# Loading K and Q in six-token runs: cast during the load, transposed head by head, written back in token order by the evacuation

## The chip, the cores and the metric

The kernel runs on one core of one Trainium2 chip. The metric is device time in microseconds (us), and each kernel is given as the median of several executions. All ratios below compare executions in the fast state; a median is taken over all executions of a run, so now and then a slow one is in it. (A slower state was seen in some executions of several of the kernels, the kernel before among them: on one chip 289.27 us in it, against 284.91 to 288.84 in its fast ones.) The engines are PE (matmul; PEld is its weight load), DVE, ACT and POOL (the vector, scalar and general engines), and SP, which here only issues DMA transfers. The kernel keeps its tiles in two on-chip memories, SBUF and PSUM. PE's results are in PSUM (`Sps`, `Ops` and `Mps` in the traces); the loads go to tiles in SBUF. A copy from PSUM to SBUF is called an evacuation.

## The reference, cut to what matters

Block-sparse attention over 4 batches, 8 heads, 768 tokens and 64 elements per head, followed by a gated MLP on the result:

```python
scores = (1 / sqrt(D)) * q @ k.T           # per batch and head, 768 x 768
# mask: blocks of 32 tokens: own block and both neighbours, the first and last
# block as rows and columns, and 3 sampled blocks for each block of queries
attn = softmax(where(mask, scores, -1e9))
x = (attn @ v)                             # heads side by side: 768 x 512
h = gelu(x @ w_in); u, w = halves of h
w = layer_norm(w) * g_ln
out = x + (u * (w_sg @ w + b_sg)) @ w_out
```

Inputs and output are float32, and q, k and v are 0.1 times a standard normal draw. The scores are therefore close to zero and the softmax close to a plain mean over the allowed tokens. A result that agrees with the reference says little about the order of the tokens in Q and K.

## The kernel before

The program is written as a list of operations with their reads and writes and a modelled duration (`dur`). A list scheduler with a model of the chip puts them in an order for each engine before the kernel is built. The program fixes the order: each engine gets its own list, with waits on semaphores.

For each batch, Q and K must end up with the head elements on the partitions (`QT`, `KT`: 128 partitions = 2 heads x 64, 768 tokens along the row), in bf16. The path is load (float32, into one of two staging buffers), cast to bf16 on POOL, six 128x128 transposes on PE into PSUM, evacuation by ACT or DVE:

```python
def load1(b, nm, c, n_, aft=()):                  # one pair of heads (c) of q, k or v
    ...                                           # batches 1-3: stg is one of the two buffers ST
    if nm == "v" or b:                            # 256-byte runs: one token of one head
        sr = SRC[nm][b, 2*c:2*c+2].rearrange("h (t p) d -> p (h t) d", p=P)
        sg = stg.rearrange("p (a d) -> p a d", d=D)
    else:                                         # batch 0, q and k: 512-byte runs, two tokens
        sr = SRC[nm][b, 2*c:2*c+2].rearrange("h (n p j) d -> p (h n) (j d)", p=P, j=2)
        sg = stg.rearrange("p (a d) -> p a d", d=2*D)
    ld = op("SP", ..., lambda e: e.dma_start(sg, sr), ...)
    ...
    eng = CAST0[nm] if b == 0 else CS1 if (b, nm) == (1, "v") else "POOL"
    op(eng, f"cs{nm}{b}.{c}", fn, ...)            # the cast, float32 -> bf16
# [...]
def tr(pe, ...):                                  # transposes of one pair of heads
    for t in range(T):                            # T = 6
        cc = u.slot * 1024 + t * P
        ins = pe.transpose(Mbf[:, cc:cc + P], n_[:, c, t, :], ident[:, :])
# [...]
def ev(x, ...):                                   # evacuation; Q on ACT and K on DVE for b > 0
    src = Mbf[:, u.slot * 1024:u.slot * 1024 + S]
    o_ = TT[:, c, 0:S]
    if b == 0:                                    # two tokens of a run lie side by side in QT/KT
        src = src.rearrange("p (n j c) -> p n j c", n=3, j=2)
        o_ = o_.rearrange("p (n c j) -> p n j c", n=3, j=2)
    return x.activation(o_, src, ACT.Copy) if ee == "ACT" else x.tensor_copy(o_, src)
```

In batch 0 a partition holds two neighbouring tokens. After the transpose these lie in two different blocks of 128 columns, so the evacuation must interleave them: it writes bf16 elements with a stride of 2 elements (4 bytes).

The softmax here doesn't subtract the row's maximum and nothing guards it: scores larger than these inputs give would overflow.

## Time and profile before

| | before |
|---|---|
| time, median of the first 3 executions (with the one beside the changed kernel: 4) | 284.9 us (283.02) |
| span of the profiled execution, granted clock | 280.6 us, 0.95 |
| DMA packets of 256 B, and what they took (mean; sum over 16 engines) | 61,440; 20.7 ns; 79.3 us |
| all DMA packets, time summed and divided by 16 engines | 199.0 us |

The last two rows are sums over the trace's packet records. Here is the head of the page of the kernel before. The first two lines give the span and the busy time of each engine with its share and its instruction count. In the others the span is cut into 40 slices of 7 us; a digit is the busy share in tenths, and PEclk is the granted clock of PE.

```profile
span 280.6 us, 8680 instructions
PE 216.9 (77%) x3525; PEld 159.9 (57%) x3525; DVE 163.8 (58%) x469; ACT 152.4 (54%) x227; POOL 112.4 (40%) x208
...
PE   0134675878776999974588998969669999999974
...
PEclk9999998779999999999689999997959999999999
DMA  8999989999969768588996794868910112320033
```

No engine is full. The DMA row is near 9 for the first third, and the PE row has two dips, near 130 and near 195 us. These are the borders between batches, where PE has to wait for the next Q and K. Busy time per engine in three stretches of 30 us shows the same (first the stretch and its length; then the busy us of PE, PEld, DVE, ACT and POOL, each with its number of instructions in parentheses; then PE's granted clock, the DMA share and GB/s. A packet is counted in the stretch in which it starts, so a DMA share can pass 1):

```profile
60.00:90.00 30.00, 24.78 (x242) 18.34 (x234) 20.02 (x61) 14.06 (x23) 13.42 (x18) 0.94 0.99 214
120.00:150.00 30.00, 19.71 (x220) 14.22 (x212) 16.28 (x53) 13.25 (x21) 16.44 (x21) 0.89 0.93 218
180.00:210.00 30.00, 22.49 (x264) 17.70 (x263) 17.59 (x53) 14.02 (x21) 17.52 (x23) 0.83 0.70 178
```

PE's waits by releaser (total us, times, longest) name the cause of those dips. `Mps L591` is the transposes, and `qn`, `kn` are the cast Q and K. The third line is the first score matmul, which waits for an evacuation. (Left out are 13.3 us for batch 0's own casts, at the start, and others.)

```profile
PE Mps L591 <- POOL qn L559: 13.0, 8, 3.0
...
PE Mps L591 <- POOL kn L559: 1.8, 2, 1.2
PE Sps L394 <- ACT QT L604: 1.7, 1, 1.7
```

The casts are late because their staging loads are late: the page has POOL idle for 34.7 us before its 12 casts of K, all of it until a load had landed:

```profile
L559 POOL CAST kn<-ST 128x768 bf16<-128x768 f32 x12 | 10.0, 830 | 34.7 <-DMA ST<-in_k_dram 34.7
```

In the page's chain of waits, which follows the last instruction back to what released it, POOL has 11% and DMA 19%:

```profile
PE 40%; DMA 19%; SPq 12%; POOL 11%; issue 10%; DVE 5%; ACT 2%; POOLq 0%
```

The instructions of the evacuation line are given as minimum/median/maximum in ns, then first and last start in us, then the shapes:

```profile
L604 ACT ACTIVATE QT<-Mps x14: 804/811/1021, 27.8 to 206.6; 128x768 bf16<-128x768 bf16 x14
L604 DVE COPY KT<-Mps x12: 516/558/558, 62.2 to 186.7; 128x768 bf16<-128x768 bf16 x12
L604 ACT ACTIVATE KT<-Mps x4: 1007/1012/1027, 15.8 to 20.7; 128x768 bf16<-128x768 bf16 x4
L604 DVE COPY QT<-Mps x2: 1004/1004/1005, 23.0 to 24.5; 128x768 bf16<-128x768 bf16 x2
```

The last two groups and two of the first belong to batch 0 and write with the 4-byte stride: 1.0 us on both engines. The others write with unit stride: 0.56 us on DVE and 0.81 on ACT.

### The profile page before, as it was taken

The page shows a single profiled execution, that of the slowest core. Times are in us where ns is not written, and L with a number is a line of the kernel's source. Part 1 is how long each engine was busy: PE and PEld are TensorE (multiplying, and loading weights), DVE is VectorE, ACT ScalarE, POOL GpSimd, SP SyncE. Part 2 cuts the span into 40 slices and gives each one's busy share as a digit, 9 for nine tenths or more (in the row PEclk, how much of TensorE's full clock was granted, in tenths as well). Part 3 has the DMA queues.
Part 4 walks back from the last instruction along what each step waited for, and adds up shares of the span by engine and source line. Part 5 has one row for each costly group of instructions (what it writes and reads, how often), then busy time and mean ns, then how long its engine had stood idle before and what let it go on. Part 6 is the DMA issues. An engine that isn't in the chain of part 4 may idle for free.

```text
span 280.6 us, 8680 instructions
## 1 busy us (share of the span) xinstructions
PE 216.9 (77%) x3525; PEld 159.9 (57%) x3525; DVE 163.8 (58%) x469; ACT 152.4 (54%) x227; POOL 112.4 (40%) x208
## 2 busy tenths in 40 slices
PE   0134675878776999974588998969669999999974
PEld 0123454766454677762466676756467777868442
DVE  6108634212986658529254897655934685557783
ACT  3471876845064657750556756745527667766000
POOL 1017863160387865125669543128674220012000
PEclk9999998779999999999689999997959999999999
DMA  8999989999969768588996794868910112320033
GB/s 155 245 279 220 231 189 283 270 204 235 263 116 238 165 148 185 130 208 214 248 208 154 143 211 100 202 165 218 265 31 3 31 45 56 127 66 0 0 114 112
DMA packets 93852, 45.43 MB, mean 162 GB/s; under 512 B 68468, under 2 KB 88084, under 8 KB 93812
## 3 DMA queue, kind: packets, MB, share of 16 engines
q1 hardware_dynamic: 86848, 34.26, 54.5%
q0 software_dynamic: 4128, 9.02, 12.8%
q10 hardware_dynamic: 2836, 1.60, 2.7%
q8 instruction: 28, 0.46, 0.7%
q14 instruction: 12, 0.10, 0.1%
HBM read 36.49 MB, written 9.55 MB: 164 GB/s over the span
## 4 chain that ended last, share of the span: by engine, by line
PE 40%; DMA 19%; SPq 12%; POOL 11%; issue 10%; DVE 5%; ACT 2%; POOLq 0%
PE Mps L394 25%; DMA ST<-in_q_dram 7%; PE Ops L394 6%; POOL VR L678 6%; PE Sps L394 5%; SPq L548 5%; DMA ST<-in_k_dram 5%; DMA scr<-VA 4%; SPq L670 3%; DMA uT<-in_k_dram 3%; DVE gt L979 2%; SPq L632 2%; POOL KR L695 2%; PE Mps L913 2%; POOL qn L559 2%
## 5 line engine op out<-in xcount | busy, mean ns | idle before, releaser
L678 POOL DMA_INDIRECT VR<-scr,IDX x47 | 46.4, 987 | 24.0 <-issue 9.0
L691 DVE COPY KR<-KT 128x128 bf16 x176 | 33.2, 256 | 9.1 <-PE Sps L394 4.7
L394 PE MATMUL Mps<-w_sgT,vh 128*128 128x384 bf16 x192 | 35.1, 327 | 0.2
L695 POOL COPY KR<-KT 128x128 bf16 x88 | 23.5, 308 | 21.2 <-PE Sps L394 21.1
L394 PE MATMUL Mps<-w_out,xg 128*128 128x512 f32 x96 | 29.5, 433 | 1.9 <-DVE xg L982 1.6
L394 PE MATMUL Mps<-w_in,xg 128*128 128x512 f32 x96 | 27.5, 432 | 3.1 <-ACT vg L937 2.1
L979 DVE SCALAR_TENSOR_TENSOR gt<-Mps,gcol,bsg 128x384 f32<-128x384 f32 x32 | 19.7, 617 | 16.2 <-PE Mps L394 15.6
L394 PE MATMUL Mps<-xg,w_in 128*128 128x384 f32 x128 | 28.3, 368 | 0.7 <-ACT uT L964 0.2
L770 ACT ACTIVATE PR<-Sps 96x1024 bf16<-96x1024 f32 (+1 forms) x24 | 22.8, 948 | 8.2 <-PE Sps L394 8.2
L997 DVE TENSOR_TENSOR x_tok<-Mps,x_tok 128x512 f32<-128x512 f32 x24 | 16.6, 690 | 16.3 <-PE Mps L394 16.0
L394 PEld LDWEIGHTS Mps<-xg,w_in 128*128 128x128 f32 x128 | 22.9, 202 | 4.4 <-ACT uT L964 1.8
L937 ACT ACTIVATE vg<-Mps 128x512 f32<-128x512 f32 x24 | 14.2, 597 | 20.0 <-PE Mps L394 18.4
L604 ACT ACTIVATE QT<-Mps 128x768 bf16<-128x768 bf16 x14 | 11.6, 839 | 23.3 <-PE Mps L591 15.3
L394 PEld LDWEIGHTS Mps<-w_sgT,vh 128*128 128x128 bf16 x192 | 17.2, 98 | 11.9 <-DVE gt L979 1.4
L559 POOL CAST kn<-ST 128x768 bf16<-128x768 f32 x12 | 10.0, 830 | 34.7 <-DMA ST<-in_k_dram 34.7
L591 PE MATMUL Mps<-ident,qn 128*128 128x128 bf16 x96 | 9.9, 252 | 17.7 <-POOL qn L559 13.0
L394 PEld LDWEIGHTS Mps<-w_in,xg 128*128 128x128 f32 x96 | 18.0, 202 | 9.0 <-ACT vg L937 3.6
L920 ACT ACTIVATE xg<-Mps 128x512 fp32r<-128x512 f32 x24 | 14.3, 594 | 15.5 <-PE Mps L913 15.3
L394 PEld LDWEIGHTS Mps<-w_out,xg 128*128 128x128 f32 x96 | 17.1, 196 | 7.3 <-DVE xg L982 2.4
L950 DVE TENSOR_SCALAR vh<-vg,lnmv,lny 128x512 bf16<-128x512 f32 x24 | 13.3, 594 | 13.2 <-POOL lny L946 13.2
L964 ACT ACTIVATE uT<-Mps 128x384 f32<-128x384 f32 x32 | 15.7, 492 | 9.7 <-PE Mps L394 9.3
L939 DVE BATCH_NORM_STATS2 lnst<-vg 128x6 f32<-128x512 f32 x24 | 16.3, 679 | 7.8 <-ACT vg L937 7.8
(98 smaller groups left out, 399.7 us busy)
## 6 DMA issues: line engine op xcount, KB each, us to landing
out_dram<-x_tok SPq DMA_DIRECT2D x20, 256.0 KB, 3.4
ST<-in_v_dram SPq DMA_DIRECT2D x12, 384.0 KB
ST<-in_k_dram SPq DMA_DIRECT2D x12, 384.0 KB
ST<-in_q_dram SPq DMA_DIRECT2D x12, 384.0 KB
VR<-scr SPq DMA_DIRECT2D x123, 32.5 KB, 2.9
scr<-VA SPq DMA_DIRECT2D x6, 390.0 KB, 6.9
w_in<-in_moe_w_in_dram POOLq DMA_DIRECT2D x1, 2048.0 KB, 9.6
VS<-scr SPq DMA_DIRECT2D x3, 650.0 KB, 7.5
```

The costliest lines, as they stand in the source:

```text
L394: return pe.matmul(o, l, r, start=start, stop=True, skip_group_check=True)
L559: fn = {"DVE": lambda x: x.tensor_copy(o4, i4), "ACT": lambda a: a.activation(o4, i4, ACT.Copy), "POOL": lambda g: g.tensor_copy(o4, i4)}[eng]
L678: return g.indirect_dma_start(out=VR[0:96, uV.slot, :, :].rearrange("p h e -> p (h e)"), out_offset=None, in_=src[:, :], in_offset=bass.In ...
L691: ins = x.tensor_copy(KR[:, c0:c0 + n, rg, 32 * j:32 * j + 32], KT[:, c0:c0 + n, bass.ds(vals["DVE", i][j][0], 32)])
L695: op("POOL", f"kp{b}.{i}{hh}", lambda x, i=i, rg=rg: x.tensor_copy(KR[:, c0:c0 + n, rg, 64:96], KT[:, c0:c0 + n, bass.ds(vals["POOL"][0][i ...
L770: return lambda a: a.activation(o, i_, ACT.Exp, scale=SCALE)
L920: return x.tensor_copy(o_, i_) if xe == "DVE" else x.activation(o_, i_, ACT.Copy)
L937: op("ACT", f"gV{b}.{tau}", lambda a: a.activation(vg[vr][:, :], Mps[:, u.slot * 512:u.slot * 512 + 512], ACT.Gelu_apprx_tanh), r=[("vp", ...
L939: op("DVE", f"bs{b}.{tau}", lambda x: x.bn_stats(lnst[:, vr, :], vg[vr][:, :]), r=[("vg", vr)], w=[("lnst", vr)], dur=0.73, prio=pr - 300)
L964: o = op("ACT", f"gU{b}.{c}{dt}", lambda a: a.activation(uT[c][:, dt, :], Mps[:, u.slot * 512:u.slot * 512 + 384], ACT.Gelu_apprx_tanh), r ...
L979: op("DVE", f"g1{b}.{c}{dt}", lambda x: x.scalar_tensor_tensor(gt[gr][:, :], Mps[:, u.slot * 512:u.slot * 512 + 384], gcol[:, dt:dt + 1], ...
L997: op("DVE", f"res{b}.{tau}", lambda x: x.tensor_tensor(x_tok[bp][:, tau, :], Mps[:, u.slot * 512:u.slot * 512 + 512], x_tok[bp][:, tau, :] ...
```

## The change

The intent is to remove what the borders wait for. A partition takes six consecutive tokens of a head, so a load reads runs of 6 x 64 x 4 = 1,536 bytes instead of 256. For batches 1 to 3 POOL issues the loads and the DMA casts to bf16 on the way; the staging buffer and POOL's cast of Q and K fall away, and Q and K can arrive an attention early. The layout on the partition is now [head, 6 tokens, 64], so each head is transposed by itself into one half of the PSUM partitions. A column block t of PSUM then holds the tokens 6p + t, and the evacuation has to put them back in token order. The scheduler also gets a table of priority offsets (`OFF`), found by an offline search of the schedule model, and new durations in the model. The core of the diff:

```diff
+OFF = { "TRk0": -456, "TRk1": -1922, ... }         # 223 entries [cut]
-                o.prio = -rk[o.idx] if RANK == 1 else o.prio - RANK * rk[o.idx]
+                o.prio = o.prio - RANK * rk[o.idx] + OFF.get(kind(o), 0)
...
-    qn = sb("qn", [P, 4, T, P], BF16)              # and kn
+    qn = sb("qn", [P, H, T, D], BF16)
...                                                 # batch 0, in load1
-            sr = SRC[nm][b, 2 * c:2 * c + 2].rearrange("h (n p j) d -> p (h n) (j d)", p=P, j=2)
+            sr = SRC[nm][b, 2 * c:2 * c + 2].rearrange("h (p j) d -> p h (j d)", j=T)
...                                                 # batches 1-3, in loads
+            if b and nm != "v":
+                if c % 2 == 0:
+                    z = c // 2
+                    dst = {"k": kn, "q": qn}[nm]
+                    o = op("POOL", f"ld{nm}{b}.{z}", lambda g, ...: g.dma_start(
+                        dst[:, 4 * z:4 * z + 4, :, :].rearrange("p h j d -> p h (j d)"),
+                        SRC[nm][b, 4 * z:4 * z + 4].rearrange("h (p j) d -> p h (j d)", j=T)), ...)
+                continue
...                                                 # transposes, batches 1-3
+                            for hp in range(2):
+                                ins = pe.transpose(Mbf[64*hp:64*hp+64, ...], n_[:, 2*c+hp, t, :], ident[:, :], tile_position=(0, 64 * hp))
...                                                 # evacuation, all batches
-                    src = Mbf[:, u.slot * 1024:u.slot * 1024 + S]
-                    o_ = TT[:, c, 0:S]
-                    if b == 0: [the 4-byte interleave]
+                    src = Mbf[:, u.slot * 1024:u.slot * 1024 + S].rearrange("p (j c) -> p j c", j=T)
+                    o_ = TT[:, c, 0:S].rearrange("p (c j) -> p j c", j=T)
-                op(ee, ..., dur=(0.85 if ee == "ACT" else 0.6) + 0.35 * (b == 0), ...)
+                op(ee, ..., dur=1.0, ...)
```

The evacuation's loop runs over t (j) outside and over the partition (c) inside, so its writes have a stride of six bf16 elements, 12 bytes. The model of the new schedule takes 1.0 us for it.

## The prediction

> **What bounds the kernel now.** No single engine: the page's busy shares are PE 77%, DVE 58%, ACT 54%, POOL 40%. In the table of engine time by stretches the DMA share is about 1.0 from 0 to 80 us, and PE works 45 of those 80: the front is DMA-bound. After 100 us PE sets the pace, except at the batch borders: it is busy 19.7 of 30 us in 120–150 and 22.5 of 30 in 180–210, and the granted clock falls to 0.75 and 0.67 there. PE's waits show why: the transposes waited 13.0 us for POOL's casts of Q and 1.8 us for those of K; POOL's casts waited for the staging loads (34.7 us for K, 16.0 for Q). The chain of waits runs through these loads and casts at 55–62, 85–91, 112–121, 133–138 and 184–206 us.
>
> **What the change does.**
> - K and Q of batches 1–3: 36,864 packets of 256 B, 20.7 ns each in the trace's packet records, 47.6 us of all 16 DMA engines. They become 6,144 packets of 1,536 B in, 768 B out. The casting weight load (1,536 B out) took 144 ns a packet; half of that is an estimate of 72 ns, 28 us in all. Batch 0's K and Q go from 512 B packets (35 ns, 13.6 us) to 1,536 B, about 9–10 us. Together 23 us of 199 us of DMA time. [...] this trace still rises from 512 B (14.5 B/ns per engine) to 2,048 B (21).
> - POOL loses 24 casts of 0.83 us (20 us) and gains 12 load issues of about 0.85 us (as the weight loads), 10 us. The two-buffer staging ring serves V alone, so K and Q can arrive an attention early.
> - Transposes: six 128-wide become twelve 64-wide in two column halves that should overlap; I allow 0 to 0.3 us for each of 24.
> - Evacuations lose their unit stride. Batch 0's strided ones show the price: DVE 1.00 against 0.56 us, ACT 1.01 against 0.81; 5.3 us of DVE and 2.4 us of ACT over 12 each. [...]
> - The new order comes from a model, so part of its promise won't appear.
>
> **On the critical path.** Front 3–5 us (first scores at 29.7 us move to about 26); 60–100 us 4–6 us; border at 120–150 us 7–8 us; border at 180–210 us 5–6 us, some of it clock. Given back: 2–4 us through slower evacuations and transposes. Net about 20 us. The last 20 us (PE and DVE alternating) stay. Floor: PE work of 210 us after a start at 27 us, front bubbles of 9 us and a tail of 5, about 251; I don't expect to reach it.
>
> Predicted: 264 us, 80% range 254 to 275. Faster by over 2%: 0.92; within 2%: 0.06; slower: 0.02.
>
> **What would show it right.** PE's waits for POOL's casts gone and not replaced by waits for the new loads; PE over 26 of 30 us at both borders, clock at least 0.95; 256 B packets down by 36,864; DMA busy time near 176 us; POOL busy down by 10 us; strided evacuations near 1.0 us; first scores near 26 us; PE busy within 5 us of 217.
>
> **What would make it wrong.** Casting loads much slower than 72 ns a packet; POOL issues that delay the gathers; V's path (load, cast, scratch write, gathers) setting the borders by itself; an order fitted to a model that stalls the in-order engines on the chip; PE instruction fetch with 144 more transposes.

Its sum: 3 to 5, 4 to 6, 7 to 8 and 5 to 6 us, less 2 to 4, about 20 us in all.

## The result

| | before | after |
|---|---|---|
| time, median of 4 executions | 283.02 us (280.63 to 284.92) | 300.62 us (300.06 to 301.39) |
| span and granted clock of the profiled execution | 280.6 us, 0.95 | 298.2 us, 0.90 |
| packets of 256 B | 61,440 | 24,576 |
| casting packets of K and Q (768 B written) | none | 6,144, 87.5 ns each |
| all DMA packets, time / 16 | 199.0 us | 176.2 us |
| evacuations of Q and K, summed over the four groups | 24.1 us | 85.4 us |

The ratio of after to before is 1.0704, with a 95% interval of 1.0651 to 1.0758: slower by 7%. Here and below, a ratio is the mean time of one kernel's fast runs over that of the other's of the same rounds, so it is not quite the ratio of the medians quoted beside it.

The head of the page after:

```profile
span 298.2 us, 8924 instructions
PE 225.6 (76%) x3669; PEld 165.8 (56%) x3669; DVE 187.2 (63%) x469; ACT 184.2 (62%) x227; POOL 101.1 (34%) x196
...
PE   0131367863488999977779999958858999999995
...
PEclk9999999995559999996559999975986999999999
DMA  8985593899993788775599471420251102420005
```

DMA and POOL are relieved as planned: POOL is down by 11 us. But ACT is up by 32 us and DVE by 23. The number of DVE and ACT instructions has not changed (469 and 227), so the same instructions have become longer. PE's dips have not gone: the one near 130 us is shallower but longer, the one near 195 us longer too, and there is a new one near 70 us. The clock falls in all of them, to 0.66 over 30 us in two. The stretches around the dips:

```profile
60.00:90.00 30.00, 17.33 (x364) 13.67 (x365) 17.49 (x42) 19.21 (x15) 7.06 (x20) 0.66 1.11 226
130.00:160.00 30.00, 22.68 (x433) 17.09 (x432) 20.97 (x45) 21.26 (x20) 10.99 (x22) 0.66 0.71 132
190.00:230.00 40.00, 30.42 (x547) 23.00 (x546) 26.58 (x59) 25.31 (x28) 12.96 (x25) 0.79 0.30 78
```

PE's waits say for what. No line with POOL's casts is left. (Batch 0's own casts, on ACT and DVE, are left out again: 16.8 us.) Instead PE waits for the evacuations (L651), which hold the PSUM buffers that transposes, scores and the MLP's matmuls write to:

```profile
PE Mps L641 <- ACT QT L651: 6.9, 5, 2.2
PE Mps L641 <- DVE KT L651: 6.7, 4, 1.9
...
PE Mps L960 <- DVE KT L651: 3.9, 3, 1.5
...
PE Mps L960 <- ACT QT L651: 3.1, 2, 1.7
PE Sps L430 <- ACT QT L651: 2.8, 1, 2.8
```

With the three smaller ones (1.9, 1.9, 0.9) these waits are 28.1 us; before, PE waited 2.9 us for evacuations. The chain of waits agrees: ACT and DVE have gone from 7% to 36%, and DMA and POOL from 30% to 9%:

```profile
PE 47%; ACT 18%; DVE 18%; DMA 9%; SPq 3%; issue 3%; ACTq 1%; POOL 0%; DVEq 0%
```

And the evacuation line itself:

```profile
L651 ACT ACTIVATE QT<-Mps x14: 2719/2744/2967, 32.5 to 222.6; 128x768 bf16<-128x768 bf16 x14
L651 DVE COPY KT<-Mps x12: 2697/2786/2867, 65.0 to 201.7; 128x768 bf16<-128x768 bf16 x12
L651 ACT ACTIVATE KT<-Mps x4: 2699/2708/2940, 15.4 to 24.2; 128x768 bf16<-128x768 bf16 x4
L651 DVE COPY QT<-Mps x2: 2694/2700/2705, 27.7 to 31.9; 128x768 bf16<-128x768 bf16 x2
```

They take 2.7 to 2.8 us, on two different engines, where the prediction (and the model of the new schedule) had 1.0. The sum is 37.6 + 31.7 + 10.7 + 5.4 = 85.4 us, 61 us more than before; the forecast was 7.7 us more. The timeline of ACT shows what this does at the first border (start, length, instruction, and in brackets the idle time before it and its releaser):

```profile
75.51 0.85 ACT L595 ACTIVATE VA<-ST 128x768 bf16<-128x768 f32 x1 [9.97 <-DMA ST<-in_v_dram]
...
76.74 10.41 ACT L651 ACTIVATE QT<-Mps 128x768 bf16<-128x768 bf16 x4
```

ACT first sits idle for V's load and then spends 10.4 us on four evacuations in a row, in which nothing else gets through.

### The profile page after: what moved, and what is told of

The parts are those of the page before. It is cut to its first block, busy times and chain, and to the rows that moved or that the text cites. A ratio compares the mean times of both kernels' runs of the same rounds, so it can differ in the third digit from the quotient of the medians.

```text
span 298.2 us, 8924 instructions
## 1 busy us (share of the span) xinstructions
PE 225.6 (76%) x3669; PEld 165.8 (56%) x3669; DVE 187.2 (63%) x469; ACT 184.2 (62%) x227; POOL 101.1 (34%) x196
## 4 chain that ended last, share of the span: by engine, by line
PE 47%; ACT 18%; DVE 18%; DMA 9%; SPq 3%; issue 3%; ACTq 1%; POOL 0%; DVEq 0%
PE Mps L430 29%; ACT QT L651 10%; DVE KT L651 7%; PE Ops L430 7%; DMA ST<-in_v_dram 6%; PE Sps L430 6%; DVE gt L1026 4%; DVE xg L1029 3%; ACT KT L651 3%; PE Mps L960 3%; DMA uT<-in_k_dram 2%; PE Mps L641 2%; ACT PW L818 2%; SPq L584 1%; DVE QT L651 1%
## 5 line engine op out<-in xcount | busy, mean ns | idle before, releaser
L742 POOL COPY KR<-KT 128x128 bf16 x88 | 22.7, 300 | 62.0 <-DVE KT L651 29.9
L651 ACT ACTIVATE QT<-Mps 128x768 bf16<-128x768 bf16 x14 | 37.6, 2800 | 8.6 <-PE Mps L638 5.7
L738 DVE COPY KR<-KT 128x128 bf16 x176 | 27.7, 243 | 10.6 <-PE Sps L430 6.8
L430 PE MATMUL Mps<-w_in,xg 128*128 128x512 f32 x96 | 30.8, 460 | 2.1 <-ACT QT L651 1.9
L651 DVE COPY KT<-Mps 128x768 bf16<-128x768 bf16 x12 | 31.7, 2784 | 0.9 <-PE Mps L641 0.9
L430 PE MATMUL Mps<-xg,w_in 128*128 128x384 f32 x128 | 26.9, 359 | 0.2
L430 PEld LDWEIGHTS Mps<-xg,w_in 128*128 128x128 f32 x128 | 21.7, 192 | 4.8 <-ACT uT L1011 2.2
L960 PE MATMUL Mps<-ident_f,x_tok 128*128 128x128 f32 x96 | 18.0, 319 | 7.3 <-DVE KT L651 3.9
L818 ACT ACTIVATE PW<-Sps,b_odd 128x512 bf16<-128x512 f32 (+1 forms) x24 | 15.7, 655 | 10.0 <-PE Sps L430 9.9
L984 ACT ACTIVATE vg<-Mps 128x512 f32<-128x512 f32 x24 | 14.6, 623 | 10.4 <-PE Mps L430 9.2
L430 PE MATMUL Ops<-VA,PW 128*64 128x65 bf16 x384 | 20.8, 209 | 0.0
L848 ACT ACTIVATE PG<-Sps 128x512 bf16<-128x512 f32 x24 | 14.0, 596 | 10.9 <-PE Sps L430 7.8
```

The source lines that it names most:

```text
L430: return pe.matmul(o, l, r, start=start, stop=True, skip_group_check=True)
L738: ins = x.tensor_copy(KR[:, c0:c0 + n, rg, 32 * j:32 * j + 32], KT[:, c0:c0 + n, bass.ds(vals["DVE", i][j][0], 32)])
L742: op("POOL", f"kp{b}.{i}{hh}", lambda x, i=i, rg=rg: x.tensor_copy(KR[:, c0:c0 + n, rg, 64:96], KT[:, c0:c0 + n, bass.ds(vals["POOL"][0][i ...
L818: return lambda a: a.activation(o, i_, ACT.Exp, bias=bias[0:p1, 0:1], scale=SCALE)
L960: ins = pe.transpose(Mps[:, cc:cc + P], x_tok[bp][:, tau, kt * P:kt * P + P], ident_f[:, :])
```

## The experiments

**The theory (A)** is that the evacuation's 12-byte write stride makes it 2.7 times as long as forecast, and that this alone turns the gain into a loss; the loads, the transposes and the order work about as meant. **The rivals** are that the searched order does not suit the chip; that the late V (the 9.97 us above) or the front sets the time; and that the loads or the extra transposes cost what was gained. Within A, the cost of one evacuation had three readings: a price for a write that falls too far from the one before it, whatever the size of the element (A1), a price for lone 2-byte writes as such (A2), or a price on the PSUM side (A3).

Chips differ: the same changed kernel took 300.6 us in the first result and 313.6 on another chip, the kernel before 283.0 and 286.5. So each ratio is to the kernel before on the same chip.

### The stride taken away from the change alone: e1_unit_write

The loop is swapped: tokens of a partition inside, so that the writes run in order and the reads from PSUM jump (256 bytes). The result is the same, element by element. Nothing else is touched, neither the order nor the modelled durations.

```diff
-  src = Mbf[...].rearrange("p (j c) -> p j c", j=T)
-  o_ = TT[:, c, 0:S].rearrange("p (c j) -> p j c", j=T)
+  src = Mbf[...].rearrange("p (j c) -> p c j", j=T)
+  o_ = TT[:, c, 0:S].rearrange("p (c j) -> p c j", j=T)
```

> Edit: the changed kernel with one thing different: the 32 evacuations of transposed Q and K run in the other loop order, so that they write the destination with unit stride and read PSUM with a stride of 256 B; same instruction count, same order of instructions on all engines, right result. Theory A (the 12-byte write stride is what costs): each evacuation falls from 2.7 us to about 1.0 us (DVE) and 0.85 us (ACT), about 56 us of DVE and ACT work go, and the time falls from 300.6 to 262-275 us, below the kernel before. Theory B (the new order of instructions and the POOL-issued loads stall the chip, and the evacuation is hidden): the evacuations fall but the time stays at 290 us or more. Theory C (any permutation of 768 elements costs this, the PSUM side too): evacuations stay at 2 us or more and the time near 300 us.

Measured: 274.34 us against 287.33, ratio 0.9534 (0.9455 to 0.9613), as theory A had it. From the profile: its busy times, its evacuation line, and PE's waits, with all those for evacuations (L651):

```profile
PE 217.3 (79%) x3669; PEld 160.4 (59%) x3669; DVE 165.4 (60%) x469; ACT 151.2 (55%) x227; POOL 101.3 (37%) x196
```

```profile
L651 ACT ACTIVATE QT<-Mps x14: 793/810/810, 25.4 to 201.2; 128x768 bf16<-128x768 bf16 x14
L651 DVE COPY KT<-Mps x12: 947/949/958, 60.0 to 187.2; 128x768 bf16<-128x768 bf16 x12
```

```profile
PE Mps L430 <- DVE gt L1026: 6.8, 1, 6.8
...
PE Mps L638 <- DVE QT L651: 4.2, 2, 3.8
...
PE Mps L641 <- DVE KT L651: 0.3, 1, 0.3
...
PE Mps L430 <- ACT QT L651: 0.3, 1, 0.3
```

ACT pays nothing for the jumps in PSUM (810 ns, as unit stride before), and DVE 0.95 us. The evacuations sum to 27.1 us (before 24.1, after 85.4), ACT and DVE are back to their busy times of before, and PE's waits for evacuations of batches 1 to 3 are below 1 us (L638 is batch 0, where 4.2 us are left; the first line is taken up at the end). PE busy is 217.3 us with the same 3,669 instructions that took 225.6 in the changed kernel, so the 144 extra transposes did not cause that rise. It came with the lower clock (0.90 against 0.96): the matmuls listed as `Mps<-w_in,xg` took 460 ns in the changed kernel and 418 here. Twelve half-wide transposes took 526 ns from the first start to the last end in most groups, six whole ones 509 in the kernel before; so two half-wide ones took about the time of a whole one, as the prediction had supposed.

### The stride added to the kernel before alone: b_slow_evac

The kernel before, with its loads, casts, transposes and order, evacuates with the change's two lines in all batches. The tokens of Q and K then come out in a wrong order. This run tells time only.

```diff
-  src = Mbf[...]; o_ = TT[:, c, 0:S]
-  if b == 0: [the 4-byte interleave]
+  src = Mbf[...].rearrange("p (j c) -> p j c", j=T)
+  o_ = TT[:, c, 0:S].rearrange("p (c j) -> p j c", j=T)
```

> Edit: the kernel before with only its 32 evacuations of Q and K written with the 12-byte stride of the change (wrong result on purpose: the tokens of Q and K come out permuted, shapes and counts are the same). Loads, casts, transposes and order are untouched. Theory A: this alone costs the kernel before about as much as the change lost against what was forecast, 20 to 35 us, so 300 to 318 us. Theory B: the evacuations hide behind the waits for loads and casts, under 8 us, so 283 to 291 us.

Measured: 321.58 us against 287.33, ratio 1.1184 (1.1095 to 1.1274). The groups of the two main evacuations (busy us, mean ns, then the idle time before them):

```profile
L601 ACT ACTIVATE QT<-Mps 128x768 bf16<-128x768 bf16 x14 | 38.3, 2735 | 19.2 <-PE Mps L394 9.6 <-PE Mps L591 9.2 <-issue 0.3
...
L601 DVE COPY KT<-Mps 128x768 bf16<-128x768 bf16 x12 | 31.9, 2773 | 6.3 <-PE Mps L591 6.2
```

Added alone it costs 34 us, within the 20 to 35 of theory A (the time passes its 300 to 318 us, as the kernel before is slower on this chip too); taken away alone it gives back 40 (see after_again and e1_again). Both directions point to the same term.

### The searched order taken away: e1_no_off

```diff
-OFF = { "TRk0": -456, ... }
+OFF = {}
```

on top of e1_unit_write.

> Edit: as e1_unit_write, and the table of searched priority offsets is emptied, so that the order is the list scheduler's own. Right result. Theory A says the search's order is worth what it is worth and no more: this run 5 to 15 us slower than e1_unit_write. Theory B (the searched order misfits the chip and is part of the loss): this run is faster than e1_unit_write by 3 us or more.

Measured: 305.58 us against 287.33, ratio 1.061 (1.051 to 1.0711), on the same chip as e1_unit_write. So the searched order is no cost: with these loads it is worth about 11 points, 31 us where 5 to 15 had been expected. This rival falls. It also means that with the new loads and the list scheduler's own order the kernel is 6% slower than before. The run does not tell what the search would have given to the old loads.

### The price of a stride by itself: micro_strides

A kernel of copies only, three of each kind, of 768 bf16 elements on 128 partitions; its output is wrong. It ran once, so its state is unknown; the means below are of three instructions each.

```python
st(t, j) = t[:, 0:768].rearrange("p (c j) -> p j c", j=j)        # writes with a stride of j elements
rd(t, j) = t[:, 0:768].rearrange("p (j c) -> p j c", j=j)        # reads in order
e.tensor_copy(st(dst, j), rd(ps, j))                             # j = 2, 3, 4, 6, 8, 16, 32
e.tensor_copy(dst as "p (c j) -> p c j", ps as "p (j c) -> p c j")    # the swapped loop
e.tensor_copy(dst as "p (c j k) -> p j c k", ps as "p (j k c) -> p j c k")    # pairs: two neighbours, then on by 12 bytes
# and the same to a float32 destination, from SBUF, and on ACT and POOL
```

> A kernel of copies alone (wrong result on purpose, zeros out): 128 x 768 bf16 elements, each case three times, one after the other, on DVE and ACT from PSUM, then from SBUF on DVE, ACT and POOL. Cases: unit stride; scattered writes at strides of 4, 6, 8, 12, 16, 32, 64 B; the swapped loop (unit-stride writes, PSUM reads at 256 B); pairs; and 4-byte elements written at 12, 16, 24 B. Theory A1 [...]: up to 8 B about 1.0 us on DVE, about 2.7 us at 16, 32 and 64 B, 12 B near that; 4-byte elements at 16 and 24 B as slow as 2-byte ones. Theory A2 [...]: 4-byte elements fast at every stride, about 1.0 us. Theory A3 (the PSUM side is at fault): from SBUF the 12-byte case is fast, and the swapped loop is as slow as 2.7 us.

(Two explanations in parentheses are cut, as no run shows the mechanism they name; the times that each reading forecast stand.)

The groups of the copies out of PSUM; in this order: DVE 16 bytes of stride, ACT 12, DVE 12, DVE 8, DVE with 4-byte elements at 16 bytes, DVE 4, DVE swapped loop (j = 6), DVE pairs, ACT pairs, ACT swapped loop, DVE unit stride:

```profile
L64 DVE COPY dst<-psf 128x768 bf16<-128x768 bf16 x3 | 10.6, 3549 | 0.1
...
L149 ACT ACTIVATE dst<-psf 128x768 bf16<-128x768 bf16 x3 | 8.1, 2715 | 0.1
L60 DVE COPY dst<-psf 128x768 bf16<-128x768 bf16 x3 | 8.1, 2703 | 0.1
...
L56 DVE COPY dst<-psf 128x768 bf16<-128x768 bf16 x3 | 5.6, 1854 | 0.1
...
L92 DVE CAST dstf<-psf 128x768 f32<-128x768 bf16 x3 | 4.5, 1502 | 0.1
...
L48 DVE COPY dst<-psf 128x768 bf16<-128x768 bf16 x3 | 3.0, 1007 | 0.1
L76 DVE COPY dst<-psf 128x768 bf16<-128x768 bf16 x3 | 2.9, 958 | 0.1
...
L84 DVE COPY dst<-psf 128x768 bf16<-128x768 bf16 x3 | 2.9, 957 | 0.1
...
L173 ACT ACTIVATE dst<-psf 128x768 bf16<-128x768 bf16 x3 | 2.5, 822 | 0.1
...
L165 ACT ACTIVATE dst<-psf 128x768 bf16<-128x768 bf16 x3 | 2.4, 810 | 0.1
...
L44 DVE COPY dst<-psf 128x768 bf16<-128x768 bf16 x3 | 1.7, 557 | 0.1
```

DVE's series of 4, 6, 8, 12 and 16 bytes is 1007, 1432, 1854, 2703, 3549 ns: each further 4 bytes cost 846 to 849 ns. At 32 and 64 bytes it is 3358 and 3485, so no rise was seen above 16. ACT has the same times within 13 ns, and POOL, from SBUF, within 28 (2729 at 12 bytes). A line fits all five points within 3 ns, worked out from them:

time ≈ 160 ns + 768 x (stride / 16 bytes) x 4.41 ns.

The product in the middle can be read as a count: the 16-byte stretches of the destination that the writes enter, counted anew in each pass. A pass of 128 elements at 12 bytes crosses 1,536 bytes, 96 stretches; six passes enter 576; 576 x 4.41 + 160 = 2,700 ns. At 4 bytes it is 192 stretches and 1,007 ns. At 16 bytes every element is in a stretch of its own, and at 32 and 64 bytes it did not become worse. The 16 is the last stride up to which the time was seen to rise (the next one tried was 32); what on the chip makes the price, the run does not show. It is a price of A1's kind, but not A1 as it was forecast: that had about 1.0 us up to 8 bytes (measured 1854 ns there), 2.7 us at 16 (3549), and 4-byte elements as slow as 2-byte ones.

A2 holds as much as A1: what costs the 4.41 ns is a 2-byte element written alone. 4-byte elements at 16 bytes took 1502 ns, about 1.75 ns for each stretch ((1502 - 160) / 768), were flat beyond (1494 at 24 bytes) and took 1168 at 12 bytes, where 576 x 1.75 + 160 gives the same. And the pairs, two bf16 neighbours written one after the other before the jump of 12 bytes, enter 288 stretches, for which the formula has 1430 ns; they took 957 on DVE, as the swapped loop, and 822 on ACT. So the formula is for lone 2-byte writes; writing in pairs might have been a second way out, untried in the kernel. Two lone writes to the same stretch did not escape: a stride of 8 bytes has two bf16 writes to each 16 bytes and took 1854 ns, twice the 958 of the swapped loop. A3 falls as a cause: with the swapped loop PSUM is read in jumps and the price is gone (ACT 810 ns, DVE 958). The source still plays a part on DVE, as the same scatter out of SBUF took 1441 ns at 12 bytes and not 2703, while ACT took 2748; why is open.

Here is also why batch 0 misled. Its 4-byte stride costs 1.0 us on both engines. DVE needs about as much in the swapped loop, where nothing is scattered (958 ns), so 1.00 against 0.56 could pass for a fixed price of leaving the plain order, one that does not grow with the stride. It was the first point of a series that rises.

### Long runs without the rest: b_long_runs and b_long_again

The kernel before with six-token runs through its own staging buffers and casts, and the swapped evacuation; its order is that of before.

```diff
-  if nm == "v" or b:
+  if nm == "v":
 ...
-  "h (n p j) d -> p (h n) (j d)", p=P, j=2      # and the matching sg
+  "h (p j) d -> p h (j d)", j=T
 ...                                              # evacuation as in e1_unit_write, all batches
```

> Edit: one part of the change alone, in the kernel before with its order of instructions untouched: K and Q of all batches are loaded in six-token runs (1,536 B packets), still by the staging loads and POOL's casts, and evacuated with the permutation in the cheap loop order (unit-stride writes). Right result. What it tells: the worth of the packet size alone. My theory (the packets are worth DMA time, the casts and staging the rest): DMA busy time falls by about 20 us as in the change, PE's waits for POOL's casts shrink from 15 us to 8 or less, and the time falls by 2 to 5%, so 268 to 279 us on a chip where the kernel before takes 284. Rival (with the old order the instructions wait in their queues for other things, and packets buy nothing): within 1% of the kernel before.

> b_long_runs once more, unaltered, because only one of its executions fell in the fast state: the kernel before in its own order, with six-token runs in the staging loads of K and Q and the cheap permuted evacuation. That one fast execution was 3.2% below the mean of the fast ones of the kernel before. Expected 0.96 to 0.975. If the packet size buys nothing in the old order either, 0.99 to 1.01.

The first run was inconclusive: 274.56 us against 284.44, but three of its four executions were slow, so there is no ratio (the one fast execution was 3.2% below the fast ones of before). The repetition on another chip gave 282.21 us against 288.22, ratio 0.9826 (0.9759 to 0.9892), with a DMA time of 174.2 us, and 5.9 us of PE's waits for POOL's casts left (4.0 for K, 1.9 for Q). That lies between the two expectations, 0.96 to 0.975 and 0.99 to 1.01. Runs of 1,536 bytes take 25 us of packet time away and, with the evacuation that they need, are worth 1.7% by themselves (1.1 to 2.4): clear of noise, but small.

### Short runs with the rest: e1_short_runs and e1_short_again

e1_unit_write, but the casting loads of batches 1 to 3 read one token at a time again, and their evacuation is plain.

```diff
-  dst[...].rearrange("p h j d -> p h (j d)"), SRC[...].rearrange("h (p j) d -> p h (j d)", j=T)
+  dst[...].rearrange("p h t d -> p (h t) d"), SRC[...].rearrange("h (t p) d -> p (h t) d", p=P)
```

> Edit: the changed kernel with the cheap evacuation and its searched order, but the casting loads of K and Q of batches 1 to 3 take the old token order, so 256 B packets again (four times as many descriptors for POOL's loads); evacuations of those batches are plain copies, so that the result is right (that alone helps: about 0.4 us on DVE for each of 12). What it tells: whether long runs matter once the loads are issued an attention early. My theory: 24,576 more and shorter packets, about 12 to 20 us more DMA busy time, most of it in the crowded first 80 us; 2 to 4% slower than e1_unit_write, so 278 to 286 us where the kernel before takes 284. Rival (loads are early enough, packet size is hidden): within 1% of e1_unit_write.

> e1_short_runs once more, unaltered: casting loads in the old token order (256 B in, 128 B out), plain evacuations in batches 1 to 3, right result. Expected 0.925 to 0.945 of the kernel before. Against e1_again it tells what the six-token runs and their permuted evacuation are worth together: Theory P 0 to 2.5% faster than e1_again.

The first gave 261.92 us against 284.44, ratio 0.9345 with a wide interval (0.9004 to 0.9686), as few of the runs of before on that chip were fast. I had expected it to be 2 to 4% slower than the version with long runs; it was not, and the expectation was wrong. (So was its count: the trace has 30,720 more packets, not 24,576, so six times as many for these loads and not four, and on one chip 42 us more packet time, not 12 to 20.) The repetition, beside the other versions on one chip, follows.

### Everything on one chip: after_again, e1_again, e1_plain_evac

after_again is the changed kernel and e1_again is e1_unit_write. e1_plain_evac is e1_unit_write with a plain, unpermuted evacuation for batches 1 to 3 (wrong token order): it shows what the permutation still costs once it is swapped.

```diff
-  src = Mbf[...].rearrange("p (j c) -> p c j", j=T)      # and o_
+  src = Mbf[...]; o_ = TT[:, c, 0:S]
+  if b == 0: [as in e1_unit_write]
```

> The changed kernel once more, unaltered, so that it and its variants share one chip. Expected 1.06 to 1.08 of the kernel before, evacuations of 2.7 us.

> e1_unit_write once more, unaltered, on the chip of the other three. Its first profile had one DVE idle stretch of 6.9 us at 100 us that no semaphore explains. If that was chance, the profile lacks it and the ratio is 0.93 to 0.945; if it belongs to this order, it is there again and the ratio is 0.95 to 0.96.

> Edit: e1_unit_write (six-token runs, casting loads) with plain evacuations, unit stride on both sides, in batches 1 to 3 (wrong on purpose: the tokens of Q and K stay in the permuted order). Long runs and fast evacuation together. Theory P (packet size is hidden once loads are early, and what e1_short_runs gained over e1_unit_write is the evacuation, 0.95 to 0.56 us on DVE, or chance): equal to e1_short_again within 1%. Theory R (long runs are worth something of their own): faster than e1_short_again by 1.5% or more. Theory S (long runs hurt): slower by 1.5% or more.

| kernel, same chip | median us | ratio to before (95%) | DMA packets / 16 |
|---|---|---|---|
| before | 286.54 | | |
| after_again | 313.58 | 1.0934 (1.0871 to 1.0996) | |
| e1_again | 273.72 | 0.9516 (0.9444 to 0.9588) | 176 us |
| e1_plain_evac | 275.06 | 0.9588 (0.9544 to 0.9633) | |
| e1_short_again | 274.47 | 0.9567 (0.9523 to 0.9612) | 218.5 us |

Two lines of the diff separate 313.58 from 273.72. Two expectations were missed: after_again lies above its 1.06 to 1.08, and e1_short_again above its 0.925 to 0.945, level with e1_again and not faster. (The profile of e1_again fell in the slow state, so its 176 us are from there; e1_unit_write had 173.9.) The last three do not differ by more than their intervals. So the swapped permutation costs nothing that can be seen, and neither do the short runs: 42 us more of packet time, once the loads cast on the way and are issued early, stay off the critical path. (Batch 0 keeps its 1,536-byte runs in all of these.)

### The mended version once more: e1_third

> e1_unit_write a third time, unaltered, beside the run above: the new order and the casting loads on top of the same long runs and the same evacuation. Two chips gave 0.953 and 0.952. Expected 0.945 to 0.96, so at most 2% below b_long_again: the casting loads and the searched order together would then be worth 1 to 2%.

Measured: 277.11 us against 288.22, ratio 0.9626 (0.957 to 0.9682), a little above what was expected, and 2% below b_long_again. Over three chips the change with the swapped evacuation is 0.9534, 0.9516 and 0.9626 of the kernel before: faster by 4 to 5%, and faster than both kernels.

One more way did not compile: letting PE write the transposes interleaved, so that the evacuation would be plain. It ran on no chip.

## Why the prediction was wrong, point by point

- **The step that failed** is the term for the evacuations: "Evacuations lose their unit stride. Batch 0's strided ones show the price: DVE 1.00 against 0.56 us, ACT 1.01 against 0.81; 5.3 us of DVE and 2.4 us of ACT over 12 each", and with it "Given back: 2–4 us". The cost was named, but its size was taken from a 4-byte stride for a 12-byte one, as if it did not grow with the stride; that was the estimate from one point. Measured: 2.7 to 2.8 us each, 61 us in sum instead of 7.7, and 34 (added alone) to 40 us (taken away alone) of time, where 2 to 4 were to be given back. The difference of two ACT values could have been a warning: ACT too was slower at 4 bytes (1.01 against 0.81 us), so the price was not one of DVE alone.
- **The DMA side was right in size.** 256-byte packets fell by 36,864 as said, the DMA time to 176.2 us (said: near 176), batch 0's 1,536-byte packets take 9.4 us (said: 9 to 10). A casting packet took 87.5 ns, the estimate was 72, so K and Q of batches 1 to 3 cost 33.6 us and not 28; that the total came out at 176 all the same is in part luck, as the packets that the change does not touch took less time than before. POOL fell by 11.3 us (said: 10).
- **But the DMA time was not worth what was put on it.** The short-run version has 42 us more of it and the same time. Long runs were worth 1.7% in the old order, where the loads still stand in the path; the casting loads, issued early, and the searched order together took another 2% off that (0.9626 against 0.9826 on one chip), and reach as much without long runs in batches 1 to 3. No run tells what the searched order would do with the old loads, so the two are not separated.
- **PE's waits for POOL's casts are gone**, as said, "and not replaced by waits for the new loads", also as said. They were replaced by waits for the evacuations, which the list did not have.
- **First scores** moved from 29.7 to 38.3 us instead of to 26: six of batch 0's eight evacuations are on ACT, and each is 1.7 us longer. With the swapped loop they start at 27.5 us.
- **The borders** did not clear in the changed kernel: PE is busy 22.7 of 30 us from 130 to 160, at a clock of 0.66. In e1_unit_write PE is busy 24.6 of 30 us at 120 to 150 and 29.3 of 30 at 180 to 210, at clocks of 0.94 and 1.00; forecast were over 26 and at least 0.95. The second came as said, the first fell a little short.
- **PE busy** rose by 8.7 us in the changed kernel (said: within 5), with the lower clock and not through the transposes; mended it is 217.3. The instruction queue, named among the risks, moved 29 packets and 0.48 MB, against 28 and 0.46 before.
- **Net of the failed term** the forecast was 264/283 = 0.933, and the mended version has 0.952 to 0.963. The remaining two to three points are not settled. Two places stand out in e1_unit_write: PE waits 6.8 us at about 100 us for a DVE operation, for whose own wait the profile finds no releaser on this core, and the load of V for batch 1 stands in the chain of waits for 19.2 us from 50.1 us on. The first was absent in e1_short_runs (span 260.1 us) and present in the same program on another chip (273.0 us). In the kept traces a stall of 6.2 to 7.1 us at this operation is in all six runs of the searched order on chips 13, 15 and 8, after_again among them, and in neither of the two others (e1_short_runs, and the changed kernel's first). Both programs that ran with and without it had ratios 2.2 to 2.3 points apart (0.9345 and 0.9567; 1.0704 and 1.0934), about 6.5 us. So it may be most of what is missing, which is not shown: one of these ratios has a wide interval, and the cause of the stall stays open.

## What to carry to other kernels

A permutation that an evacuation had to make was far cheaper on its PSUM reads than on its SBUF writes: 0.81 us on ACT and 0.95 on DVE against 2.7 to 2.8 each, and here two lines were worth 40 of 314 us. A price read from one stride must not be carried to another without a second point: for lone 2-byte writes the copies went from 1007 ns at 4 bytes to 2703 at 12 and 3549 at 16, and 128x768 bf16 elements written in pairs at 12 bytes took 957. And when a price at the one point that you have could belong to an engine or to the writes, look at another engine that does the same work: here ACT, too, was slower at 4 bytes (1.01 against 0.81 us).
